# Turning x into token rows: TensorE transposes replaced, from the third batch row on, by a VectorE block transpose and small transfers on two queues

**Chip, cores, metric.** One core of one Trainium2 chip. The metric is the device time of one execution in microseconds (us), as a median over executions; lower is better. Batch rows are counted 1 to 8 in the text and in the prediction. In the code `b` runs from 0 to 7, and in some of the expectations below "row 2" and "row 3" are `b`, so rows 3 and 4 of the text.

## The reference

```python
# q, k, v: (8, 8, 576, 64) float32; tau = 0.02
scores = (q @ k.T) / 8                                   # per batch row and head
scores = where(scores >= max(scores) - tau, scores, -1e9)
attn = softmax(scores) @ v                               # sum + 1e-9 in the denominator
x = attn.transpose(0, 2, 1, 3).reshape(8, 576, 512)      # tokens x channels
u = x + (relu(x.T @ w_tok1) @ w_tok2).T                  # token layer, w_tok1 576x256
out = u + relu(u @ w_ch1) @ w_ch2                        # channel layer, w_ch1 512x1536
```

## The kernel before

Work goes in 144 units of 128 queries of two heads. Three units make a group: their weights e (the softmax weights; from row 2 on) are turned by VectorE in 32x32 blocks into `T`, and sixteen transfers on SP (the sync queue) put the blocks in place in `eT`. Then the value products of the group run on TensorE. A batch row has 18 units and six groups.

```python
def turn_blocks(u):
    ...
    nc.vector.transpose(out=T[:, :, place, :]..., in_=e...)              # L365
    if place == GU - 1:
        eT = work.tile([P, GU, 4, NK * 32], F32, tag="eT", bufs=1, ...)
        for a in range(4):
            for i in range(4):
                nc.sync.dma_start(out=eT[32*a:32*a+32, :, i, :], in_=T[32*i:32*i+32, a, :, :])   # L374
```

The value products leave x with channels on partitions (`xT`). The token layer needs tokens on partitions, so x is turned once more, on TensorE:

```python
def turn_x(t):                                                           # 5 per batch row
    for p in range(NP):
        nc.tensor.transpose(out=ps[0:M, p, :], in_=xT[:, p, ...], identity=ident)   # L432
    nc.scalar.copy(out=x_sb[0:M, t, :], in_=ps...)                                  # L433
...
steps = [(0.44, lambda t=t: turn_x(t)) for t in range(NT)]
steps += [... tok1 ...]; steps += [... tok2 ...]
```

Steps of the token and channel layers are queued (`push`) when the last value products of a row are issued, and a bit of that queue is worked off in each unit (`fill`). It is what TensorE does between the scores of one unit and the next. In this document the **room** of a group is the TensorE work that stands between the turning of its last e and its value products.

## Time and profile before

| | before |
|---|---|
| time, median (3 runs) | 1378.74 us (1378.43 to 1379.69) |
| TensorE busy | 96% of the span |
| VectorE, ScalarE busy | 43%, 42% |
| value products' wait for e, whole span | 3.3 us |

The prediction shows the page's lines. Two more are needed for the comparison. In the PE timeline (start, duration, what, idle time just before and what ended it) this is the fourth group of row 3; the sixteen value products take 2.78 us after a wait of 0.78:

```profile
377.00 0.87 PE L408 MATMUL pv<-eT,vl 128*64 128x384 f32 x4 [0.78 <-DMA eT<-T]
377.67 2.78 PE L413 MATMUL pv<-eT,lv 128*64 128x384 f32 x16
380.38 1.24 PE L302 MATMUL sc<-kT,qT 64*128 64x288 f32 x8
```

And in the windows view (stretch, busy time of PE, PEld, DVE, ACT, POOL with their counts, then PEclk, the granted clock) TensorE is never idle in these 8 us and has its full clock:

```profile
384.00:392.00 8.00, 8.00 (x33) 4.89 (x33) 5.44 (x9) 3.62 (x9) 3.13 (x8) 1.00 0.54 130
```

### The profile page before, as it was taken

How to read it: one execution, taken by the hardware profiler on the slowest of the kernel's cores; microseconds unless marked ns; L12 is line 12 of the kernel's file. 1: busy time of each engine (PE TensorE's matmuls, PEld its weight loads, DVE VectorE, ACT ScalarE, POOL GpSimd, SP SyncE). 2: the span in 40 equal slices, each digit the busy share in tenths (PEclk: the TensorE clock that was granted, in tenths of full speed). 3: DMA queues.
4: the chain of work that ended last, by engine and by line, in shares of the span. 5: the costliest groups of instructions: out<-in, count | busy, mean ns of one | idle time of the engine just before them, and what ended most of it. 6: DMA issues, size and time to landing. Idle time of an engine off the chain costs nothing.

```text
span 1375.1 us, 17691 instructions
## 1 busy us (share of the span) xinstructions
PE 1322.7 (96%) x6226; PEld 817.9 (59%) x6226; DVE 588.2 (43%) x1017; ACT 581.8 (42%) x1288; POOL 356.0 (26%) x683
## 2 busy tenths in 40 slices
PE   6877799999999999999999999999999999999998
PEld 3444465646565666565665567565656576575675
DVE  6788875445444443434244444434333453201000
ACT  5666654454445444443434444353333444120110
POOL 4555653222222222222122222222121222100000
PEclk9988999999999999999999999999999999999999
DMA  5434655454544354433344435434433442400000
GB/s 121 98 96 125 183 142 124 100 123 98 122 109 114 82 121 94 113 88 95 77 100 94 113 77 123 106 83 98 103 87 75 107 103 63 115 1 16 8 11 21
DMA packets 278871, 128.20 MB, mean 93 GB/s; under 512 B 200896, under 2 KB 271552, under 8 KB 278784
## 3 DMA queue, kind: packets, MB, share of 16 engines
q1 hardware_dynamic: 150176, 111.06, 32.0%
q10 hardware_dynamic: 128608, 16.01, 7.3%
q8 instruction: 50, 0.82, 0.3%
q14 instruction: 37, 0.30, 0.1%
HBM read 43.25 MB, written 9.44 MB: 38 GB/s over the span
## 4 chain that ended last, share of the span: by engine, by line
PE 85%; DVE 7%; DMA 2%; SPq 2%; ACT 1%; issue 1%; POOL 1%; ACTq 0%; DVEq 0%; POOLq 0%
PE c L486 26%; PE c L470 26%; PE sc L302 11%; PE pv L413 9%; PE t L441 5%; PE t L448 3%; PE pv L408 3%; DVE mx L307 2%; SPq L374 2%; PE tx L432 1%; PE c L482 1%; DMA eT<-T 1%; PE tr L353 1%; DVE wc L205 1%; ACT e L317 1%
## 5 line engine op out<-in xcount | busy, mean ns | idle before, releaser
L307 DVE TENSOR_REDUCE mx<-sc 128x1 f32<-128x576 f32 x288 | 204.5, 751 | 487.9 <-PE sc L302 487.5
L470 PE MATMUL c<-xT,wc 128*128 128x256 f32 (+1 forms) x1920 | 399.4, 362 | 2.1 <-DVE xT L452 1.2
L486 PE MATMUL c<-wc,g 128*128 128x512 f32 x864 | 390.5, 597 | 0.0
L470 PEld LDWEIGHTS c<-xT,wc 128*128 128x128 f32 x1920 | 334.5, 191 | 71.5 <-issue 27.6
L308 POOL TENSOR_SCALAR bias<-mx,toff 128x1 f32<-128x1 f32 x288 | 82.8, 288 | 799.3 <-DVE mx L307 742.3
L317 ACT ACTIVATE e<-sc,bias 128x576 f32<-128x576 f32 x288 | 199.6, 739 | 162.0 <-POOL bias L308 161.4
L486 PEld LDWEIGHTS c<-wc,g 128*128 128x128 f32 x864 | 157.8, 190 | 175.7 <-issue 174.0
L471 ACT ACTIVATE g<-c 128x256 f32<-128x256 f32 (+1 forms) x240 | 86.7, 362 | 334.1 <-PE c L470 317.9
L324 ACT ACTIVATE e<-e,ntau 128x576 f32<-128x576 f32 x288 | 220.7, 771 | 0.0
L335 POOL TENSOR_SCALAR e<-e,rr 128x576 f32<-128x576 f32 x288 | 215.6, 761 | 15.8 <-DVE rr L332 4.3
L302 PE MATMUL sc<-kT,qT 64*128 64x288 f32 (+1 forms) x1280 | 196.6, 447 | 11.1 <-DVE kT L284 7.1
L365 DVE STREAM_TRANSPOSE T<-e 128x1152 f32<-128x1152 f32 x126 | 172.1, 1366 | 6.3 <-DMA eT<-T 2.6
L302 PEld LDWEIGHTS sc<-kT,qT 64*128 64x128 f32 (+1 forms) x1280 | 107.4, 184 | 98.3 <-issue 59.1
L413 PE MATMUL pv<-eT,lv 128*64 128x384 f32 (+1 forms) x1024 | 136.8, 409 | 0.0
L413 PEld LDWEIGHTS pv<-eT,lv 128*64 128x64 f32 x1024 | 76.1, 138 | 51.0 <-issue 43.6
L491 DVE COPY o<-c 128x512 f32<-128x512 f32 x36 | 24.9, 692 | 177.5 <-PE c L486 177.5
L418 ACT COPY xT<-pv 128x384 f32<-128x384 f32 (+1 forms) x56 | 21.0, 401 | 157.5 <-PE pv L413 157.5
L448 PE MATMUL t<-w,a 128*128 128x288 f32 x256 | 75.2, 421 | 7.2 <-DVE xT L452 5.3
L441 PE MATMUL t<-x_sb,w 128*128 128x512 f32 x160 | 72.1, 598 | 0.0
L448 PEld LDWEIGHTS t<-w,a 128*128 128x128 f32 x256 | 45.6, 191 | 32.2 <-issue 11.4
L452 DVE TENSOR_TENSOR xT<-xT,t 128x288 f32<-128x288 f32 x64 | 28.2, 446 | 80.5 <-PE t L448 80.0
L324 ACT ACTIVATION_READ_ACCUMULATOR e<-e,ntau 128x1 f32 x288 | 56.5, 196 | 0.0
(44 smaller groups left out, 554.7 us busy)
## 6 DMA issues: line engine op xcount, KB each, us to landing
eT<-T SPq DMA_DIRECT2D x672, 108.0 KB, 2.2
scratch<-in_moe_w_ch_dram SPq DMA_DIRECT2D x24, 512.0 KB, 3.7
lv<-in_v_dram SPq DMA_DIRECT2D x32, 288.0 KB, 3.3
out_dram<-o SPq DMA_DIRECT2D x36, 256.0 KB, 2.2
lk<-in_k_dram ACTq DMA_DIRECT2D x111, 72.0 KB, 2.6
lq<-in_q_dram ACTq DMA_DIRECT2D x106, 72.0 KB, 2.3
lq<-in_q_dram SPq DMA_DIRECT2D x22, 72.0 KB, 3.2
lk<-in_k_dram SPq DMA_DIRECT2D x17, 72.0 KB, 3.3
```

The lines of the kernel that those rows point to most:

```text
L302: nc.tensor.matmul(sc[h][rows, f, 0:HS], lhsT=qT[r, cols], rhs=kT[r, HS * f : HS * f + HS], start=True, stop=True)
L307: nc.vector.tensor_reduce(out=mx[:, c], in_=sc[h][:, :, 0:HS], axis=AX.XY, op=ALU.max)
L317: nc.scalar.activation(out=eh, in_=sc[h][:, :, 0:HS], func=AF.Prelu, bias=bias[:, h : h + 1], scale=SCALE, alpha=STEEP)
L324: nc.scalar.activation(out=eh, in_=eh, func=AF.Exp, bias=ntau, accum_out=rs[:, h : h + 1])
L335: nc.gpsimd.tensor_scalar(out=eh, in0=eh, scalar1=rr[:, h : h + 1], scalar2=1.0, op0=ALU.mult, op1=ALU.mult)
L365: nc.vector.transpose(out=T[:, :, place, :].rearrange("p a (c x) -> p c a x", c=NK), in_=e.rearrange("p (c a x) -> p c a x", c=NK, a=4))
L413: nc.tensor.matmul(to[r], lhsT=lv[:, j, :], rhs=e[j], start=False, stop=(c == NI - 1), skip_group_check=True)
L441: nc.tensor.matmul(ps, lhsT=w1[:, t, P * m : P * m + P], rhs=x_sb[:, t, :], start=(t == 0), stop=(t == NT - 1))
L448: nc.tensor.matmul(ps, lhsT=s["a"][:, m, P * c : P * c + P], rhs=w2[:, m, HS * f : HS * f + HS], start=(m == 0), stop=(m == NTK - 1))
L470: nc.tensor.matmul(ps, lhsT=wc1[:, j, c, :], rhs=uT[:, c, GR * i : GR * i + n], start=(c == 0), stop=(c == NCC - 1))
L471: nc.scalar.activation(out=s["g"][:, j, 0:n], in_=ps, func=AF.Relu)
L486: nc.tensor.matmul(flat, lhsT=s["g"][:, j, P * t : P * t + P], rhs=wc2[:, j, :], start=False, stop=(j == NJ - 1), skip_group_check=True)
```

## The change

Intent: take the 120 transposes of x for rows 3 to 8 off TensorE, which sets the time. VectorE turns x in 32x32 blocks, as it does e; sixteen transfers for each half row put the blocks in place. Eight go on SP ahead of the next group's e, eight on ScalarE's queue, four in each of two units. The token steps are queued two units later.

```diff
+    def turn_x_blocks(b, w):
+        xt = work.tile([P, S // 32 * 64], F32, tag="xt", bufs=1, ...)
+        nc.vector.transpose(out=xt..., in_=xTs[b][:, 2*w : 2*w+2, o : o+S]...)      # L437 in the kernel after
+    def move_x(b, w, xt, eng, blocks):
+        for a in blocks:
+            for i in range(4):
+                eng.dma_start(out=x_sb[32*a : 32*a+32, 0:n, P*i+64*w : P*i+64*w+64],
+                              in_=xt[32*i : 32*i+32, a::4, :])                      # L450
...
-        steps = [(0.44, lambda t=t: turn_x(t)) for t in range(NT)]
+        steps = [] if x_in_blocks(b) else [(0.44, lambda t=t: turn_x(t)) for t in range(NT)]
...
+        if moves and u == moves[0][0] + 1:
+            xts = turn_x_blocks(*moves[0][1:])
+            move_x(*moves[0][1:], xts, nc.sync, (0, 1))       # ahead of turn_blocks, hence of e
...
+        if moves and u > moves[0][0]:
+            at, b, w = moves[0]
+            move_x(b, w, xts, nc.scalar, (u - at + 1,))
+            if u == at + 2:
+                moves.pop()
+                if w:
+                    push(b)                                    # was: in values_due, two units earlier
```

Cut: the columns of `x_sb` and of `a` are stored in another order, by strided writes of ScalarE; the old steps interleaved with the new ones are counted from the end; the pool of small tiles has 5 buffers instead of 6, because six no longer fit beside `xt`.

## The prediction

> **What bounds the kernel now.** I read the page first: busy shares, the slices, the groups. TensorE is at nine tenths or more from the seventh slice to the last but one.
>
> ```profile
> PE 1322.7 (96%) x6226; PEld 817.9 (59%) x6226; DVE 588.2 (43%) x1017; ACT 581.8 (42%) x1288; POOL 356.0 (26%) x683
> ...
> PE   6877799999999999999999999999999999999998
> ```
>
> No other engine passes 43%, so TensorE's own instructions set the time and each taken away is worth its spacing, as long as nothing new makes TensorE wait. The windows view by row says it more sharply: in the fourth batch row's stretch TensorE is busy 165.00 of 165 us.
>
> ```profile
> 460.00:625.00 165.00, 165.00 (x819) 104.34 (x819) 71.28 (x122) 75.29 (x173) 41.49 (x88) 1.00 0.46 103
> ```
>
> Next, what a transpose of x costs. In the groups its mean is 277 ns, but these times overlap. The PE timeline of the last row gives the spacing: from the start of four transposes to the start of what follows is 0.43 us (1207.77 to 1208.20, 1209.93 to 1210.37), 0.109 us each.
>
> ```profile
> 1207.77 0.60 PE L432 MATMUL tx<-ident,xT 128*128 128x128 f32 x4
> 1208.20 1.89 PE L470 MATMUL c<-xT,wc 128*128 128x256 f32 x8
> 1209.93 0.60 PE L432 MATMUL tx<-ident,xT 128*128 128x128 f32 x4
> 1210.37 1.89 PE L470 MATMUL c<-xT,wc 128*128 128x256 f32 x8
> ```
>
> Last, how close the transfers of e are to being late, because the change puts others ahead of them. The SP timeline of the group in which x of the third row will first move, and the PE timeline of the same time:
>
> ```profile
> 363.14 11.56 SPq L374 DMA_DIRECT2D eT<-T  x16
> ```
>
> ```profile
> 358.82 1.20 PE L302 MATMUL sc<-kT,qT 64*64 64x288 f32 x16
> 362.72 1.24 PE L302 MATMUL sc<-kT,qT 64*128 64x288 f32 x8
> 369.24 1.24 PE L302 MATMUL sc<-kT,qT 64*128 64x288 f32 x8
> 377.00 0.87 PE L408 MATMUL pv<-eT,vl 128*64 128x384 f32 x4 [0.78 <-DMA eT<-T]
> ```
>
> The sixteen issues take over 10 us of SP (0.602 us each, 0.645 from start to start), land 2.2 us after issue, and the value products already wait 0.78 us for them. In the waits view of SP there is a second tie: e's transfers wait for q's transfers on ScalarE's queue, though they share no data. They share the few semaphores of the DMA queues.
>
> ```profile
> SPq L374 <- DMA lq<-in_q_dram: 51.8, 22, 4.8
> SPq L374 <- DMA eT<-T: 31.1, 32, 2.5
> ```
>
> (Total us, times, longest.)
>
> **What the Trainium skill says.** (1) "TensorE: Matmul & The Clock Gate", section "PE-mode transpose": a full 128x128 transpose goes to PSUM and needs a copy after it; about 275 ns in one kernel's context. The trace agrees on that duration (median 273 ns), but spacing among other work is 109 ns, and that is what a removed one returns. (2) "VectorE: DVE Perf Modes", section "The three transpose paths": VectorE transposes 32x32 blocks only. The trace shows such a one at 128x1152 in 1.37 us (L365), with sixteen transfers to put the blocks in place. (3) "DMA: Bandwidth & Descriptors", section "Issuing engines are not separate DMA queues": issuing on several engines saves only the sequencer's time, which it calls usually small. Here it is not: 16 x 0.645 us is most of two units of work. (4) "Perfetto Trace Analysis", section "DMA Instruction — HWDGE (DVE, Sync)": the profiled DMA window is the issue, and the generator of descriptors is locked meanwhile. No line of before shows by itself how much SP and ScalarE hold each other up.
>
> **The change part by part.**
> Removed: for rows three to eight, 6 x 20 = 120 transposes on TensorE, 120 x 0.109 = 13.1 us, all on the path. Also 30 ScalarE copies x 0.585 = 17.6 us, beside the path, and some 0.5 us of TensorE's waits for them.
> Added: 12 transposes on VectorE, shaped like L365's: 12 x 1.37 = 16.4 us, at 43% load; hidden, but each stands ahead of a transpose of e. 192 transfers, 96 on SP and 96 on ScalarE, each 32x4 or 32x5 pieces of 256 bytes. That is 27,648 packets on 278,871 and 7 MB on 128: bandwidth is no matter, issue is. I take 0.645 us each on SP, as for e; q's take 0.32 to 0.51, so 0.5 is possible.
> Moved: x's eight SP transfers stand directly ahead of one group of e, in 11 of the 42 groups. The token steps of a row come two units later, so the units there have other lengths.
> Layout: the strided writes of ScalarE's copies and of `a` change neither counts nor element sizes; zero.
>
> **Is e now late?** Count from the first scores of the unit in which the group's last e is turned. In the timeline above, e's first issue is 363.14 - 358.82 = 4.3 us later (VectorE maxima 1.4, small ones, transpose 1.4); this held in the other ten groups too. Then 8 x 0.645 = 5.2 for x, 15 x 0.645 = 9.7 to the start of the last e, 2.2 to land, 0.3 to the product: it can start at 21.6 us. TensorE gets there after three units, whose length I added up from the new order on TensorE with spacings of before (scores 1.17 a unit, a first-layer step 1.77, a second-layer part 2.63, token steps 4.39 and 1.02):
> - row 3, fourth group: 17.1 us of work, so late by 4.5 (now about 1);
> - row 4, first group: 19.7 (it was 22.0; the later push leaves the previous quota in force). The last e shares its semaphore with a q transfer issued on ScalarE 4.0 us into the third unit, 13.3 us after the start: 13.3 + 4.0 + 2.2 for its landing, + 2.2 + 0.3 = 22.0; late by 2.3;
> - row 4, second group: no x of its own, but its room falls from 21.0 to 17.9 while a k transfer on ScalarE still holds it to 20.8: late by 2.8;
> - row 4, fourth group: 19.0 against 22.2: late by 3.2;
> - rows 5 and 7, fourth groups: 23.7, but the ninth e waits for a k transfer behind ScalarE work that ends 9.1 us into the next unit: 25.2, late by 1.5 each;
> - rows 6 and 8, fourth groups: 21.5 against 21.6 and 22.3: late by 0.1 and 0.8;
> - the first groups of rows 5 to 8: 22.8 or 23.3 of room: not late.
> Sum 16.7 us; about 1.5 us of such waits of before fall in the same groups, so 15 us new.
> Does the token layer wait for x? In the middle x lands about 4 us before its first product, which stands behind three older steps. At the end eight transfers on ScalarE are split by an activation; the last lands some 17 us after the last value product starts, the token product comes at 18.3. Not late, barely.
> Sum: 1378.7 - 13.1 - 0.5 + 15 = 1380. At 0.5 us per x issue it is about 1379.
>
> **Rivals.** (a) *The gain stays*: e isn't late, since x's small transfers issue fast and e's semaphores come free early. For it: 30 of the 42 groups of before have over 1 us of slack, and the long rows have 4 to 9. Against it: the short groups above. Time 1365 to 1367. (b) *Waits of e eat the gain*, my own account: 1372 to 1384. (c) *ScalarE's queue is the new trouble*: with q's and k's two, four x transfers a unit hold it for some 3 us, in order, and each waits for a semaphore which may be held by an e transfer on SP; activations come late, then the two PSUM buffers of the channel layers run out. For it: ScalarE waits for q and k in the trace already (13.7 us in total before `g`). Against: issues mostly pass while Exp runs, and ScalarE is at 42%. Time 1385 to 1400. (d) *VectorE delays the adds of the token layer*: 12 x 1.37 us at most, if each were met in full; two buffers hide most of it; under 3 us.
>
> **Range and chances.** My account gives 1380, (a) 1366. My stalls rest on issue times of larger transfers and on rooms added up without feedback, and they err to the long side if issue is quicker; so I put the point at 1377. The 8 in 10 range reaches from (a) to a moderate (c): 1365 to 1391. Faster by over 2% would need less than 1351, twice what the removed work is worth: 0.02. Slower by over 2%, above 1406, needs (c) in full: 0.04. Within 2%: 0.94.
>
> **What would show it right or wrong.** Right: the transposes' count falls from 160 to 40 and TensorE's busy time by some 13 to 18 us; the value products' wait for e grows from 3.3 us to 10 to 20, found in the fourth group of rows 3 and 4 and the first of row 4; SP shows x and e as one run of 15 us or more. Wrong: no such wait and a time near 1366 (issue of x quicker than 0.645, or rooms longer); a wait of channel or token products for `g` or of tok1 for x (rival c, or x itself late); x issues far above 0.65 us, which would take the time past 1390.

## The result, and the profile after

| | before | after |
|---|---|---|
| median, same rounds (6 runs each) | 1379.42 us | 1400.70 us (1395.89 to 1407.53) |
| ratio | | 1.0152, 95% interval 1.0121 to 1.0182 |
| again, with later experiments (11 and 6 runs) | 1380.16 us | 1398.11 us (1396.68 to 1401.65), ratio 1.0124 |
| TensorE transposes of x | 160 | 40 |
| value products' waits ended by transfers | 3.3 us | 26.6 us |

A ratio is the mean time of one kernel's runs over that of the other's of the same rounds, so not quite the ratio of the medians. The change costs 1.2 to 1.5%: within 2%, but outside the range of 1365 to 1391.

The page after. TensorE has 120 instructions less to do, yet the span is 24 us longer; three of the 35 us slices fall to 8, at 385, 455 and 525 us, where the first changed rows are. The busy time falls by 5.2 us only, and not by the 13 to 18 that the prediction gave as a sign, because the value products became longer (L413: 144.9 us against 136.8).

```profile
PE 1317.5 (94%) x6106; PEld 808.8 (58%) x6106; DVE 603.4 (43%) x1029; ACT 564.5 (40%) x1258; POOL 354.1 (25%) x683
...
PE   6877799999989898999999999999999999999998
```

The SP timeline of the kernel after, in the fourth group of row 3 and in that of row 8. The eight transfers of x (L450) go first, and e (L374) starts 6.49 and 7.10 us after the first of them:

```profile
369.04 6.31 SPq L450 DMA_DIRECT2D x_sb<-xt  x8
375.53 10.70 SPq L374 DMA_DIRECT2D eT<-T  x16
...
1153.75 5.11 SPq L450 DMA_DIRECT2D x_sb<-xt  x8
1160.85 11.17 SPq L374 DMA_DIRECT2D eT<-T  x16
```

The PE timeline of the kernel after, in the fourth groups of rows 3, 4 and 8. Each time TensorE has run out of room, waits, and then does the same value products in more time than the 2.78 us of before:

```profile
388.05 1.55 PE L408 MATMUL pv<-eT,vl 128*64 128x384 f32 x4 [5.74 <-DMA eT<-T]
389.36 4.49 PE L413 MATMUL pv<-eT,lv 128*64 128x384 f32 x16
393.78 1.24 PE L302 MATMUL sc<-kT,qT 64*128 64x288 f32 x8
...
536.93 1.55 PE L408 MATMUL pv<-eT,vl 128*64 128x384 f32 x4 [4.55 <-DMA out_dram<-o]
538.24 3.45 PE L413 MATMUL pv<-eT,lv 128*64 128x384 f32 x16
541.62 1.24 PE L302 MATMUL sc<-kT,qT 64*128 64x288 f32 x8
...
1173.88 0.98 PE L408 MATMUL pv<-eT,vl 128*64 128x384 f32 x4 [2.54 <-DMA eT<-T]
1174.58 4.44 PE L413 MATMUL pv<-eT,lv 128*64 128x384 f32 x16
```

(At 536.93 the wait is put down to an output transfer, which a value product doesn't read; the name is that of a semaphore's last event, and SP issues that output directly behind e.)

The same 8 us in the windows view after. TensorE is busy for half of them, and its clock is 0.63 on average:

```profile
384.00:392.00 8.00, 3.95 (x14) 1.73 (x16) 0.00 (x0) 0.00 (x0) 0.00 (x0) 0.63 0.45 122
```

The trace's clock records after the first rows say it directly: before, one stretch of half clock (3.4 us, at 150); after, stretches at 147, 386 (6.8 us), 461, 536 and 1174 (3.4 us each). The last four are those that begin around a wait of 2.5 us or more. From the start of the value products to the next scores took 3.38 us before; in these four groups 5.73, 5.05, 4.69 and 5.06 us. That is 2.35 + 1.67 + 1.31 + 1.68 = 7.0 us lost to the clock alone.

The waits view after (engine and line, what it waited for, total us, times, longest). TensorE's waits for transfers (with 2.9 us for a k transfer, 26.6 us), and two of ScalarE's that look bad and will turn out to cost nothing:

```profile
ACT g L508 <- DMA x_sb<-xt: 27.6, 8, 4.1
...
ACT e L317 <- DMA x_sb<-xt: 22.7, 6, 4.9
...
PE pv L408 <- DMA eT<-T: 15.9, 8, 5.7
...
PE pv L408 <- DMA out_dram<-o: 7.8, 3, 4.6
```

### The profile page after: what moved, and what is told of

The parts are those of the page before. It is cut to its first block, busy times and chain, and to the rows that moved or that the text cites. A ratio compares the mean times of both kernels' runs of the same rounds, so it can differ in the third digit from the quotient of the medians.

```text
span 1399.5 us, 17639 instructions
## 1 busy us (share of the span) xinstructions
PE 1317.5 (94%) x6106; PEld 808.8 (58%) x6106; DVE 603.4 (43%) x1029; ACT 564.5 (40%) x1258; POOL 354.1 (25%) x683
## 4 chain that ended last, share of the span: by engine, by line
PE 79%; DMA 5%; SPq 5%; DVE 5%; ACT 3%; issue 1%; POOL 1%; ACTq 1%; DVEq 0%; POOLq 0%
PE c L507 24%; PE c L523 23%; PE sc L302 10%; PE pv L413 9%; PE t L473 5%; SPq L374 4%; PE t L485 4%; PE pv L408 3%; DMA eT<-T 2%; DVE mx L307 2%; DMA lk<-in_k_dram 1%; ACT e L317 1%; PE c L519 1%; DMA scratch<-in_moe_w_ch_dram 1%; SPq L450 1%
## 5 line engine op out<-in xcount | busy, mean ns | idle before, releaser
L413 PE MATMUL pv<-eT,lv 128*64 128x384 f32 (+1 forms) x1024 | 144.9, 426 | 0.0
L413 PEld LDWEIGHTS pv<-eT,lv 128*64 128x64 f32 x1024 | 81.5, 144 | 54.0 <-issue 40.6
L408 PE MATMUL pv<-eT,vl 128*64 128x384 f32 (+1 forms) x256 | 48.1, 451 | 30.7 <-DMA eT<-T 15.9
```

The costliest lines, as they stand in the source:

```text
L408: nc.tensor.matmul(to[r], lhsT=vl[:, r], rhs=e[NI], start=True, stop=False, skip_group_check=True)
L413: nc.tensor.matmul(to[r], lhsT=lv[:, j, :], rhs=e[j], start=False, stop=(c == NI - 1), skip_group_check=True)
```

## The experiments

The theory: x's transfers on SP make e late in groups with little room; TensorE waits, and afterwards runs at half clock for a while. Rivals: ScalarE's queue; VectorE's new transposes; the later queueing of the token steps; the smaller pool. "Before" was run in the same rounds each time (medians 1380.2 to 1381.5 us).

### Without the transfers, and with each half of them

Edits of the kernel after, one or two lines each. The first three give a wrong result, because x isn't moved or only half of it.

```diff
no_moves, act_only:
-            move_x(*moves[0][1:], xts, nc.sync, (0, 1))
no_moves, sp_only:
-            move_x(b, w, xts, nc.scalar, (u - at + 1,))
both_ways (all transfers stay, TensorE's transposes come back):
-        steps = [] if x_in_blocks(b) else [(0.44, lambda t=t: turn_x(t)) for t in range(NT)]
+        steps = [(0.44, lambda t=t: turn_x(t)) for t in range(NT)]
```

> The changed kernel with all 192 transfers of x left out (rows three to eight read a stale x, a wrong result on purpose); VectorE's transposes and the later push stay. Theory A (the transfers make e late, and TensorE then waits and loses clock): no wait of value products for e over 4 us in all, no half-clock stretch after 160 us, time 1363 to 1369, which is before less the 13.7 us of removed transposes. Rival B (the later push and the shorter rooms for e cost the time, whatever moves): e stays late in the fourth group of rows 3 and 4 and the time stays above 1380. Rival C (VectorE's twelve transposes delay e and the adds): above 1375.

> The changed kernel without ScalarE's 96 transfers (wrong result on purpose); SP's 96 stay ahead of e. If standing ahead of e on SP is the main cost, most of the loss is back: waits for e in rows 3 and 4 of 2 to 4 us, 1375 to 1390. If it is mostly the semaphores that e shares with ScalarE's transfers of x: under 1371.

> The changed kernel without SP's 96 transfers (wrong result on purpose); ScalarE's 96 stay. If e's ties to ScalarE's transfers and ScalarE's own waits are the main cost: 1380 or more. If SP's place ahead of e is: 1363 to 1371.

> The changed kernel with TensorE's 120 transposes and ScalarE's 30 copies of x put back, so x is written twice with the same values. It measures what the removed work is worth in place: after plus 13 to 15 us, 1412 to 1418, if TensorE is still the bound between the waits for e; less than 8 us more if the waits for e swallow part of it, since the added work gives e more room.

| | median us | ratio to before (95%) |
|---|---|---|
| no_moves | 1372.94 | 0.9946 (0.9913 to 0.9978) |
| sp_only | 1400.62 | 1.0129 (1.0096 to 1.0162) |
| act_only | 1373.93 | 0.9948 (0.9916 to 0.9980) |
| both_ways | 1413.68 | 1.0230 (1.0194 to 1.0266) |

SP's half of the transfers does the damage: 1.0129 - 0.9946 of 1380 us is 25 us. That is more than was expected (1375 to 1390). ScalarE's half does none that shows: act_only is within 0.3 us of no_moves on average, give or take 6 (both lie some us above the 1363 to 1369 and 1363 to 1371 that the theory expected); its waits for x, 50 us in the kernel after, pass beside the path. The PE timeline of sp_only shows the wait of row 3 again, with the slow products behind it:

```profile
384.99 1.55 PE L408 MATMUL pv<-eT,vl 128*64 128x384 f32 x4 [5.05 <-DMA eT<-T]
386.30 4.45 PE L413 MATMUL pv<-eT,lv 128*64 128x384 f32 x16
```

Putting the transposes back made it 13 us longer (1413.68 against 1400.70; 1.0230 - 1.0152 of 1380 is 11, and the two intervals leave 4 to 17), which agrees with the predicted 13.1. VectorE's twelve transposes are in all of these kernels, in no_moves too, so they aren't the loss. But no_moves gains 7.5 us and not 13.6, and falls between what its three theories expected. One long wait is left in its PE timeline (and in that of act_only), in the second group of row 4, and behind it another stretch of half clock:

```profile
473.26 0.91 PE L408 MATMUL pv<-eT,vl 128*64 128x192 f32 x4 [3.33 <-DMA lk<-in_k_dram]
```

No transfer of x is there to blame for it; a later run asks whether the later queueing is.

### The smaller pool

The kernel before with `bufs=5` in the pool of small tiles.

> The kernel before with five instead of six buffers in the pool of small tiles, nothing else. Every kernel of the changed family reached row 2 some 2 to 6 us later than before in its profile, though its program there differs in this alone. If the buffer is the cause: 1382 to 1386, 3 to 6 us slower than before. If that difference is the spread of single executions: within 1 us of before.

Measured: 1379.72 us, ratio 0.9994 (0.9972 to 1.0015). The pool isn't the cause. Its profiled run also began 2.8 us later than that of the kernel before from the first units on; so differences of this size at the start are spread between executions. From the third value products of row 3 to the end the two profiles take 1019.4 and 1019.6 us. This stretch leaves the start out, and it is used again below.

### x elsewhere in the queues

x_behind: all sixteen transfers on SP directly behind e. x_act: all sixteen on ScalarE's queue, four in each of four units. Both are correct; the push waits for the last of them.

```diff
x_behind:
-        if moves and u == moves[0][0] + 1:        # (ahead of turn_blocks)
-            xts = turn_x_blocks(*moves[0][1:]); move_x(*moves[0][1:], xts, nc.sync, (0, 1))
+        ... the same behind turn_blocks, with (0, 1, 2, 3); push at u == at + 3
x_act:
-            move_x(*moves[0][1:], xts, nc.sync, (0, 1))
-            move_x(b, w, xts, nc.scalar, (u - at + 1,))
-            if u == at + 2:
+            move_x(b, w, xts, nc.scalar, (u - at - 1,))
+            if u == at + 4:
```

> The changed kernel with all sixteen transfers of x on SP, directly behind e's sixteen, none on ScalarE's queue, and the token steps one unit later still. Correct result. If place ahead of e is what costs (sp_only and act_only say so): e is late in the fourth groups no more, no half-clock stretch there, 1366 to 1374. If 192 transfers cost by their number on SP wherever they stand: over 1390.

> The changed kernel with all sixteen transfers of x on ScalarE's queue, four in each of four units, token steps two units later. Correct result. act_only moved half of them at no cost; if ScalarE's queue has the room: 1368 to 1376, with ScalarE's waits for x's transfers doubled to some 90 us and still off the path. If its blocking reaches TensorE: over 1380, with waits of channel products for g.

x_behind was a miss: 1385.70 us, ratio 1.0044 (1.0015 to 1.0072). The waits of the fourth groups are gone, but others came a group later: its waits view has the value products waiting 4.8 us for e and 5.5 us for a q transfer (on whose semaphore e's last ones depend), and the scores 7.8 us for ScalarE (before: 3.9). So x on SP directly behind e doesn't win either. How much of its loss comes from the issues and how much from the push, one unit later still, was not weighed apart. x_act is **faster than both kernels**, by 0.5% against before: 1374.04 us, ratio 0.9946 (0.9932 to 0.9961), ScalarE's waits for x 67 us and not the expected 90, no stretch of half clock after the first rows, and no wait of the value products for a transfer over 1.6 us.

### More room in the groups that were late

The kernel after, with more of the queued work in the three units before the value products (`fill` 0.75 instead of 0.4).

```diff
+                roomy.update((u + 1, u + 2, u + 3))
-            fill(0.4)
+            fill(0.75 if u in roomy else 0.4)
```

> The changed kernel, x still ahead of e on SP, but in the three units from x's turn to the value products TensorE gets 0.35 of a unit's quota more of channel and token steps, which are then missing elsewhere. By the new order, room in the fourth group of row 3 grows from 19.0 to 20.2 us, of row 2 from 17.1 to 22.3, of the first of row 3 from 19.7 to 24.5; the second group of row 3 stays at 17.0. If lateness is need less room: the waits at rows 2 (fourth) and 3 (first) go, some 12 us with their half clock, the other two stay: 1378 to 1392. If room doesn't matter and x ahead of e costs by contention: 1398 to 1404 as the changed kernel.

Measured: 1395.91 us, ratio 1.0107 (1.0085 to 1.0129), between the two expected ranges. In the fourth group of row 3 the wait went from 5.74 to 0.24 us and the products took their 2.78 us again:

```profile
389.92 0.87 PE L408 MATMUL pv<-eT,vl 128*64 128x384 f32 x4 [0.24 <-DMA eT<-T]
390.59 2.78 PE L413 MATMUL pv<-eT,lv 128*64 128x384 f32 x16
...
539.93 1.54 PE L408 MATMUL pv<-eT,vl 128*64 128x384 f32 x4 [5.36 <-DMA eT<-T]
541.23 3.67 PE L413 MATMUL pv<-eT,lv 128*64 128x384 f32 x16
```

So in row 3 the room decides, as the theory has it, and in row 4's first group the wait fell from 2.89 to 1.83 us. The work taken early is missing later, though: row 4's fourth group still waits (5.36 us), and new waits of 3.0 and 4.5 us stand at 588 and 866 us.

### The half clock by itself, the later queueing by itself, and fewer units for x

busy_wait fills the four longest waits with useless products, so that TensorE doesn't stand idle; after_again is the kernel after unaltered, beside it. no_moves_early is no_moves with the push at its old place (again a wrong result). x_act_2 is x_act with eight transfers in each of two units.

```diff
busy_wait (in values, ahead of the value products):
+    BUSY = {(2, 2, 0): 4, (3, 0, 0): 1, (3, 0, 1): 1, (3, 2, 0): 4}
+        for _ in range(BUSY.get((b, p0, g), 0)):
+            nc.tensor.matmul(whole, lhsT=ident, rhs=wc2[:, 0, :], start=True, stop=True, ...)
no_moves_early:
+                if p0 == NP - 2: push(b)          # in values_due, as before (cut: the later push is out, xT is held for VectorE)
x_act_2:
+            move_x(b, w, xts, nc.scalar, (2 * (u - at) - 2, 2 * (u - at) - 1))   # push at at + 2
```

> The changed kernel, with useless work put in the four longest waits for e: four products of 128x512 (0.87 us each in the second layer) just ahead of the value products of the fourth group of row 3 (wait 4.3 us) and of row 4 (4.6 us), and one ahead of the first and second groups of row 4 (1.5 us each); their results are overwritten. Some 8.7 us of useless work, all inside waits. If the half clock after the waits is a cost of its own (theory): the half-clock stretches near 386, 461 and 536 us vanish, and the time falls by 3 to 8 us against the changed kernel (part of it comes back as longer waits, because the groups in between lose the room that slow work gave them). If only the waits cost and the low clock is harmless: no change, or longer by up to 3 us.

> The changed kernel once more, unaltered, as the measure for the run with useless work on the same chip. Both theories: ratio to the kernel before 1.010 to 1.020, half-clock stretches after 380 us again, 15 us or more of waits of the value products.

> The changed kernel without any x transfer, and with the token steps queued as early as in the kernel before, not two units later (wrong result on purpose). Theory that the later queueing costs some 5 us at the second group of row 4: that wait and its half clock (near 473 us without transfers) vanish, time 1365 to 1369, ratio 0.988 to 0.992. Rival, that the later queueing costs nothing: as without transfers before, ratio 0.994 to 0.996.

> All sixteen transfers of x on ScalarE's queue as in the best version so far, but eight in each of two units, so that the token steps are queued two units earlier (as in the changed kernel, later than in the kernel before). If the later queueing is what the best version still loses: ratio 0.990 to 0.994. If eight transfers in one unit hold ScalarE up so that TensorE feels it: ratio 0.996 or above, with waits of the scores for e or of the channel products for g of more than 10 us.

| | median us | ratio to before (95%) |
|---|---|---|
| busy_wait | 1393.60 | 1.0090 (1.0066 to 1.0115) |
| after_again | 1398.11 | 1.0124 (1.0101 to 1.0147) |
| no_moves_early | 1367.23 | 0.9904 (0.9884 to 0.9924) |
| x_act_2 | 1402.07 | 1.0160 (1.0133 to 1.0187) |

**busy_wait** does more work and takes 4.5 us less than after_again (the means leave 1 to 8). The fourth group of row 3 in the PE timelines of after_again (first two lines) and busy_wait: instead of 4.98 us of idle time 1.97, and products at 2.78 us.

```profile
384.89 1.55 PE L408 MATMUL pv<-eT,vl 128*64 128x384 f32 x4 [4.98 <-DMA eT<-T]
386.19 5.13 PE L413 MATMUL pv<-eT,lv 128*64 128x384 f32 x16
...
378.92 3.60 PE L399 MATMUL pv<-wc,ident 128*128 128x512 f32 x8
384.48 0.87 PE L412 MATMUL pv<-eT,vl 128*64 128x384 f32 x4 [1.97 <-DMA eT<-T]
385.15 2.78 PE L417 MATMUL pv<-eT,lv 128*64 128x384 f32 x16
```

The half-clock stretches at 384 and 534 us of after_again are gone; the one at 455 to 459 stayed, where only one product had been added, and one is new at 1008, behind a wait of 1.99 us where nothing had been added. From the start of the value products to the next scores, busy_wait is 3.0 us shorter in the fourth group of row 3 and 1.7 us in that of row 4, and the two profiles part by less than 0.1 us in the groups between. (Later, where both do the same work, busy_wait loses 1.7 us at 1008 and wins 3.7 in the fourth group of row 8, whose wait happens to be shorter.) This shows the half clock as a cost of its own, caused by TensorE's idleness.

**no_moves_early** gains 13.2 us (0.0096 of 1380), the whole of the predicted gain, and its wait in the second group of row 4 is gone. The later queueing therefore costs 0.9946 - 0.9904 of 1380, 5.8 us, with intervals that leave 1 to 11; from the third value products of row 3 to the end the two profiles differ by 3.5 us (1010.1 and 1006.6).

**x_act_2** was meant to win that back and loses 28 us against x_act. In ScalarE's timeline seven issues of x stand in a row, and the unit's first activation starts after 7.52 us of idle time:

```profile
369.25 7.22 ACTq L450 DMA_DIRECT2D x_sb<-xt  x7
376.52 1.37 ACT L317 ACTIVATE e<-sc,bias 128x576 f32<-128x576 f32 x2 [7.52 <-DMA x_sb<-xt]
```

TensorE waits for it, and the scores after that take 2.92 instead of 1.24 us; products of the channel layer wait for `g` 15.3 us in total (x_act: 4.2):

```profile
377.32 2.92 PE L302 MATMUL sc<-kT,qT 64*128 64x288 f32 x8 [3.15 <-ACT e L317]
```

So rival (c) is a real danger at eight transfers a unit; at four, as in the change, it costs nothing that these runs show.

## Why the prediction was wrong

**What held.** TensorE bounds, and the removed transposes are worth some 13 us (no_moves_early: 13.2, interval 10 to 16). The waits stand in the groups it named, and rival (b), waits for e, is what happened; rival (a) is what no_moves_early shows without transfers. VectorE's transposes (12 x 1.36 us) are hidden. The layout's term of zero holds: ScalarE's writes of `a` have a mean of 597 ns in both kernels.

**The step that failed** is the one that ends "Sum 16.7 us; about 1.5 us of such waits of before fall in the same groups, so 15 us new". The mechanism of the waits was right. The sum was too small in two ways: each wait was mis-sized, and the price of the clock behind a wait was missing. (Of before's waits only 0.78 us, not 1.5, stand in the groups of the list.)

*Each wait was longer than its term.* Waits in us, predicted and in the profile of the kernel after:

| group | predicted | measured |
|---|---|---|
| row 3, fourth | 4.5 | 5.74 |
| row 4, first | 2.3 | 2.89 |
| row 4, second | 2.8 | 2.87 |
| row 4, fourth | 3.2 | 4.55 |
| rows 5 and 7, fourth | 1.5 and 1.5 | 1.81 and 1.53 |
| rows 6 and 8, fourth | 0.1 and 0.8 | 1.58 and 2.54 |
| sum | 16.7 | 23.5 |

The mis-sized terms are the issues on SP, of x ("8 x 0.645 = 5.2 for x") and of e ("15 x 0.645 = 9.7 to the start of the last e"). From the first x to the first e it took 5.3 to 7.1 us in the eleven places, 5.99 on average, so 0.75 us each. The median of one issue is 0.60 us as assumed, but in most places one of the eight lasted 0.8 to 1.6 us, or a gap came before e. e's own sixteen took 10.7 to 13.8 us against the 10.3 of the working. In row 3 this makes 1.3 + 0.4 = 1.7 us more, where the wait was 1.24 us above its term; in row 4's fourth group x was in time (5.31) and e took 11.91. The trace of before could have told: its forty-two groups of e took 10.3 to 15.1 us, 0.74 us from start to start on average, waits for semaphores included, against the median of 0.645, and the line that the prediction shows has 11.56. The prediction shaded the other way: it said its stalls "err to the long side", if issue is quicker, and put the point 3 us below its own sum. Why some issues are slow stays open: 10 of the 12 of x on SP that lasted over 0.78 us overlap an issue on ScalarE's queue, but so do 52 of the 84 others, and sp_only still has six of them, with 5.62 us from x to e.

*A wait costs more than its length.* The prediction had no term for the clock, though its own line with 1.00 in the clock column stood next to the argument. The Trainium skill, "TensorE: Matmul & The Clock Gate", section "Part 1: The HAM clock gate (the "warmup" mystery)", says that TensorE's clock is halved when it has been idle over a window of some 3.4 us, that the windows run freely, and that it takes a busy window to come back. The trace agrees: stretches of 3.4 or 6.8 us at 0.5 behind four of the waits, 7.0 us lost, and busy_wait, which lost less by working more. Only the whole idle window is not what it shows (last section).

The sum, mended: 1378.7 - 13.1 - 0.5 + (23.5 - 0.8) + 7.0 = 1395, and about 0.8 us for short waits in groups that had no term (0.98, 0.41 and 0.37 us, less 0.93 in before). The change is then worth 16.9 us. From the third value products of row 3 to the end, which is the stretch that it touches, the profiles take 1019.6 us before and 1038.1 and 1039.2 after, so 18.5 and 19.6 us more; the other 6.0 and 2.7 us by which they part stand earlier, where before_small5, a kernel no slower than before, lost 3.0. Of the 18.5 us of the profile whose waits are listed, 1.6 us stay open.

**Not weighed apart: the later queueing.** Its 5.8 us were inside the prediction's rooms ("the later push leaves the previous quota in force", and the 2.8 us of row 4's second group), but it was taken as given with the moves. It is a cost of its own. That it also limits x_act, whose push comes two units later still, was not shown.

## What to carry to other kernels

- On a bound engine, count a new wait as its length and then look at the clock behind it: here four of the five waits of 2.5 to 5.7 us were followed by products that lost another 1.3 to 2.4 us. Useless work in a wait that can't be avoided paid here, by 4.5 us.
- Transfers ahead of a critical one on the same queue cost their issue time, and the slow issues among them count, not the median: take the mean, or the whole run of issues, from the trace. Try the transfers on a queue that nobody waits for, in portions: four per unit on ScalarE were free here, eight were not.
- Where queued work fills the time of a wait, delaying the queue moves waits to other places; test the delay by itself.

## What the Trainium skill lacked or had wrong

- "TensorE: Matmul & The Clock Gate", Part 1: its table of the two states puts the half clock after at least one idle window of about 3.4 us. Here waits shorter than that were enough: after 2.89 us at 461 and 2.54 us at 1174 a stretch of 3.4 us at half clock followed, while 1.81 us at 696 and 2.87 us at 487 left the clock as it was. The clock records give the windows: the four stretches of the kernel after begin 22, 22 and 187 times 3.41 us apart. Laid on this grid, the wait at 487 is split into 0.83 and 2.04 us. Over all fourteen traces after 160 us, 35 of the 36 drops follow a window in which TensorE's records leave 1.9 us or more idle (the other 1.3), and only two windows with as much (2.04 and 2.05) are not followed by a drop. So about 2 us idle within one window was the limit in these runs, worked out from them alone. The price in a kernel that has its full clock otherwise after 160 us was 7.0 us in four groups.
- "DMA: Bandwidth & Descriptors", section "Issuing engines are not separate DMA queues": it calls the sequencer's time for issuing usually small against the transfer. Here 24 issues on SP took 17 us (369.04 to 386.23) and decided the result: the eight of x on SP cost 25 us (sp_only against no_moves), the same number on ScalarE's queue nothing (act_only).
- "TensorE: Matmul & The Clock Gate", section "Part 4: PE-mode transpose": its duration of 275 ns isn't what a removed transpose returns. 120 of them returned about 13.2 us (no_moves_early), 0.11 us each.
- No page read here says how long single issues may stick: the median of x's on SP is 0.60 us, the longest 1.63 us.
